# Attention and a two-layer MLP on one Trainium2 core: the first batch's second layer with three output chunks at once

## The chip, the cores and the metric

The kernel runs on one core of a Trainium2 chip. The metric is device time in microseconds (us), from start to end of the execution; lower is better. The engines concerned are TensorE (PE in the profile; its weight loads are PEld), VectorE (DVE), ScalarE (ACT), GpSimd (POOL) and SyncE (SP), which here issues DMAs. Each works through its own instructions in the order in which the program was written; they meet through semaphores.

## The reference, cut to what matters

```python
# q, k, v: (8 batches, 12 heads, 448 rows, 64)
q_n, k_n = rmsnorm(q, g_q), rmsnorm(k, g_k)
attn = softmax(q_n @ k_n.T / 8)
a = attn @ v
x = a.transpose(0, 2, 1, 3).reshape(8 * 448, 768)
h = x @ w_in                  # w_in  (768, 2048), float64
g = h - tanh(h)
return g @ w_out              # w_out (2048, 768), float64
```

The weights arrive as float64, the rest as float32. The kernel has to make float32 weights out of pairs of 32-bit words.

## The kernel before, in words

**Slots.** Attention is cut into 48 steps, one for each batch and pair of heads (six steps to a batch). A "slot" holds the work of one step s and work ahead for later ones: the softmax sums of s (`totals`), the scores of s + 1, the values of s, the transposes of q and k of s + 2 (`turn`), the norms of s + 3. The MLP is a Python generator that yields once per matmul; a slot calls `run` between its parts, and `run` draws as many MLP matmuls as the slot's share of time allows. What is drawn between two parts of a slot stands there in every engine's queue. Batch 0's first layer is drawn in slots 6 to 8, its second layer in slots 9 to 11, and batch 1's first layer begins in slot 12. In slots 6 to 11 (`early_slot`) the order is: `totals(s)`, the scores of s + 1 for key chunks 0 and 1, a quarter of the slot's matmuls, `turn(s + 2)`, a quarter, the last key chunk, `values(s)` and `divide(s)`, then four eighths of the matmuls with the softmax additions `add(s + 1)`, `add_last(s + 1)`, then `norm(s + 3)` and `norm_q(s + 3)` after them.

**The chain around `turn`.** The scores, sums, values and turns share five PSUM banks in rotation. In these slots the first bank that `turn` takes is the one that `totals` filled; it is free when DVE has taken the reciprocal of the sums (L701). The second bank that `turn` takes held the first scores; it is free when ACT has taken their exponential (L575). That exponential stands in ACT's queue behind `norm_q` (L454), which needs a power computed by POOL (L144) from what DVE reduced in `norm` (L142, L143).

**Weights.** There are 32 pieces: 0 to 15 of w_in, 16 to 31 of w_out (16 to 23 for output columns 384 to 767, two matrix rows of 128 each, in order; 24 to 31 for columns 0 to 383). A piece is loaded (L289 for w_in, L293 for w_out) into one of three raw buffers and rounded in three steps: two ACT instructions (L71, L72), three DVE instructions (L78, L79, L82), two POOL instructions (L92). `weight(to)` starts pieces up to the number `to`: it issues the ACT step of piece n and, with it, the DVE and POOL steps of piece n - 1, and then the load of a later piece. So DVE rounds a piece when the next one is started, and the list that gives `to` for each matmul of the MLP sets where in DVE's queue that work stands. In the first layer each product also catches up on the piece before, if it starts none.

**The first layer of batch 0** is 28 products (four sets of seven, Strassen's scheme), each of six matmuls of 128x128 by 128x224. Before product i, `weight(due[i])` is called: `due` rises from 8 pieces to 16 over products 0 to 13, and to 24 over products 14 to 27. When the four pieces of a set are rounded, four DVE sums (L356) are queued, one before each product.

**The second layer of batch 0** (`project_first`) is 96 matmuls of 128x128 by 128x448: six output chunks of 128 columns, each a sum over 16 rows of w_out. They are done chunk by chunk (chunks 3, 4, 5, 0, 1, 2), with f, the matrix row, innermost. Number them m = 0 to 95. Each slot draws 32 of them, 8 + 8 + 4 + 4 + 4 + 4. Three PSUM banks named `mm` are used in turn. At the end of a chunk ACT copies the bank (L1335), DVE turns it (L960), and half a chunk later four DMAs store it (L965). Pieces 24 to 31 start at m = 5, 11, 17, 23, 29, 35, 41, 47. At m = 52, 56, ... 80 DVE forms the Strassen sums of w_out (`combine_w_out`, L380 to L383, in two of six ring slots), which SP copies to DRAM four matmuls later (L387). At m = 84 and 86 `ring_load` fetches the first four weight tiles of batch 1 (L426) into the ring.

**What SP's queue holds.** All loads, stores and copies to DRAM, in program order. An entry that waits holds back the ones after it.

Of the kernel before, what the change touches and what calls it, by code (L numbers as in the profile page):

```python
# [67 lines left out]
def round_weight_a(nc, raw, dst):  # L68

    lo, hi = raw[:, :, 0], raw[:, :, 1]  # L70
    nc.scalar.activation(dst, hi.bitcast(F32), AF.Abs, scale=2.0**-16)  # L71
    nc.scalar.mul(lo, lo.bitcast(U32), 2.0**-29)  # L72
# [74 lines left out]
def bounded_path(tc, ctx, q, k, v, moe_w_in, moe_w_out, out, g_col, ident, ones, half_ones, neg_half, early):  # L147
# [17 lines left out]
    nc = tc.nc  # L165
    B, H, S, D = q.shape
    DFF, DM = moe_w_out.shape
    P = 128
    CP = S // NCH
    NP = H // 2  # L170
    CD, CF = DM // P, DFF // P
# [5 lines left out]
    EARLY, PIECES = 8, 2 * CF  # L177
    HS = S // 2
    HC, HF = CD // 2, CF // 2
    SETS = CF // 4  # L180
# [8 lines left out]
    def pool(name, **kw):  # L189
        return ctx.enter_context(tc.tile_pool(name=name, **kw))  # L190
# [18 lines left out]
    def bank_of(name):  # L209

        turns[name] += 1
        return banks[name][turns[name] % len(banks[name])]

    def mm_bank():
        return bank_of("mm")
# [48 lines left out]
    def w_out_row(f, i):  # L264
        return w_half[i][f // 2][:, f % 2]
# [35 lines left out]
    def weight_dst(n):  # L301
        return weight_piece(n)[2].rearrange("p f n -> p (f n)")
# [11 lines left out]
    def load_weights(to):  # L314

        while done[0] < min(to, PIECES) and place_free(done[0]):
            weight_load(done[0])
            done[0] += 1

    def weight(to):  # L320

        while done[1] < min(to, PIECES):
            n = done[1]
            keep_step(0, {CF - 4: 0, CF: 1, CF + HF: SETS - 1}.get(n, -1))
            round_weight_a(nc, raws[n], weight_dst(n))
            settle(n)
            done[1] = n + 1
            load_weights(n + (3 if n < EARLY - 3 else 4))
            if kept[1] < kept[0] and n >= 4 * kept[0] + 2:
                keep_weights()  # L330
            keep_step(2)
        if done[1] == PIECES:
            settle(PIECES)

    def settle(to):
        for n in range(done[2], to):
            round_weight_b(nc, raws[n], weight_dst(n))
            finish_weights(n + 1)
# [22 lines left out]
    def keep_weights():  # L361
        j = kept[1]
        to_keep.extend((j, p) for p in ORDER)
        kept[1] = j + 1
# [3 lines left out]
    def keep_step(count, all_of=-1):  # L368
        while to_keep and (count > 0 or to_keep[0][0] <= all_of):
            j, p = to_keep.pop(0)  # L370
            nc.sync.dma_start(out=w_in_dram[j, p].rearrange("p (f n) -> p f n", f=2), in_=built(j, p))
            count -= 1

    def combine_w_out(f):

        a11, a21 = (w_out_row(f, i) for i in range(2))
        a12, a22 = (w_out_row(f + HF, i) for i in range(2))
        t = [ring_slot() for _ in range(2)]
        s3, s1, s2, s4 = (t[i // 2][:, i % 2 * HALF : (i % 2 + 1) * HALF] for i in range(4))
        nc.vector.tensor_tensor(out=s1, in0=a21, in1=a22, op=ALU.add)  # L380
        nc.vector.tensor_tensor(out=s3, in0=a11, in1=a21, op=ALU.subtract)
        nc.vector.tensor_tensor(out=s2, in0=s1, in1=a11, op=ALU.subtract)
        nc.vector.tensor_tensor(out=s4, in0=a12, in1=s2, op=ALU.subtract)  # L383
        late["keep"].append(lambda: [keep_factors(3 + 2 * i, 2, f, t[i]) for i in range(2)])

    def keep_factors(n, count, f, src):
        nc.sync.dma_start(  # L387
            out=w_out_dram[:, n : n + count, :, f, :].rearrange("p k c d -> p (k c) d"),
            in_=src[:, : count * HALF].rearrange("p (k d) -> p k d", d=P),
        )  # L390

    def keep_w_out(n):

        if not CF <= n < PIECES:
            return
        f, i, src = weight_piece(n)
        if f >= HF or i == 0:
            blk = i + 1 if f >= HF else 0
            for r in range(2):
                keep_factors(blk, 1, f % HF + r, src[:, r])  # L400
# [3 lines left out]
    def ring_slot():  # L404
        n = slots[0] % SLOTS
        slots[0] += 1
        return ring[:, n * SLOT : (n + 1) * SLOT]
# [11 lines left out]
    def ring_load(to):  # L419

        for n in range(len(ring_tiles), min(to, len(ring_steps))):
            b, layer, j, p = ring_steps[n]
            t = ring_tiles[ring_steps[n]] = ring_slot()
            if layer == 0:
                assert kept[1] > j
                nc.sync.dma_start(out=t[:, : 2 * HALF], in_=w_in_dram[j, p])  # L426
            elif layer == 2 and p == 0:
                nc.sync.dma_start(out=t, in_=w_out_dram[:, BLOCKS[j], HC - 1].rearrange("p f d -> p (f d)"))
            elif layer == 2:
                n = min(2 * HB, 7 * HB - 2 * (p - 1) * HB)  # L430
                at = 2 * (p - 1) * HB
                nc.sync.dma_start(out=t[:, :n], in_=inner_dram[j][:, at : at + n])
            else:
                nc.sync.dma_start(out=t, in_=w_out_dram[:, BLOCKS[p], j].rearrange("p f d -> p (f d)"))
# [371 lines left out]
    late = {}  # L806


    due = [EARLY + (CF - EARLY) * (m + 1) // (7 * SETS // 2) for m in range(7 * SETS // 2)]
    due += [CF + HF * (m + 1) // (7 * SETS // 2) for m in range(7 * SETS // 2)]  # L810
    assert len(due) == 7 * SETS and due[-1] == CF + HF

    def part(name):
        if name == "th" and "blocks" in late:
            late["turn"] = (late.get("turn", 0) + 1) % 3
            if late["turn"] == 0:
                return late["blocks"].tile([P, 2, HS], F32, name="th_more")
        return tp.tile([P, 2, HS], F32, name=name)
# [134 lines left out]
    def store(b, n, y, o=None):  # L953

        if o is None:
            o = part("th").rearrange("p f s -> p (f s)")
        nc.vector.transpose(out=o, in_=y if b >= FIRST else y.rearrange("r (c p) -> r p c", c=NCH))  # L960

        def issue():
            for i in range(P // BL):
                d = n * P + i * BL
                nc.sync.dma_start(  # L965
                    out=out[b * S : (b + 1) * S, d : d + BL].rearrange("(j t) d -> t j d", t=BL),
                    in_=o[i * BL : (i + 1) * BL].rearrange("t (j d) -> t j d", d=BL),
                )

        late["out"].append([1 if b >= PAIRED else 2, issue])  # L970
# [33 lines left out]
    def step_out(by=1):  # L1004
        for entry in late["out"]:
            entry[0] -= by
        while late["out"] and late["out"][0][0] <= 0:
            late["out"].pop(0)[1]()
# [290 lines left out]
    def project_first(b):  # L1299

        g = late["g"]
        for fn in late["todo"]:
            fn()
        late["todo"] = []
        keep_step(0, SETS - 1)
        took = 4 * S / ENGINE_NS
        for m in range(CD * CF):
            k, f = m // CF, m % CF
            n = (k + HC) % CD
            if f == 0:  # L1310
                bank = mm_bank()
            if f == CF // 2:
                step_out(2)
            if k < HC:
                weight(CF + HF + HF * (m + 1) // (HC * CF))
            elif m < HC * CF + 2:
                keep_w_out(PIECES - 2 + m - HC * CF)
            elif (m - HC * CF) % 4 == 0 and m - HC * CF <= 4 * HF:
                for fn in late["keep"]:
                    fn()  # L1320
                late["keep"] = []
                combine_w_out((m - HC * CF) // 4 - 1)
            elif m == CD * CF - 12:
                ring_load(2)
                for fn in late["keep"]:
                    fn()
            elif m == CD * CF - 10:
                ring_load(4)
            nc.tensor.matmul(  # L1329
                bank[:, :S], lhsT=w_out_row(f, n // HC)[:, n % HC * P : (n % HC + 1) * P], rhs=g[:, f, :],  # L1330
                start=(f == 0), stop=(f == CF - 1),
            )
            if f == CF - 1:
                y = part("s2").rearrange("p f s -> p (f s)")
                nc.scalar.copy(out=y, in_=bank[:, :S])  # L1335
                store(b, n, y)
            yield took
        wp_stack.close()
        late["blocks"] = pool("blocks", bufs=1)
        late["second"] = pool("second", bufs=1)  # L1340
        late["tg"] = single_stack.enter_context(tc.tile_pool(name="tg", bufs=1))
        late["inner"] = inner_steps()
# [534 lines left out]
```

## Time and profile before

| | us |
|---|---|
| median of 3 runs | 1346.47 (1345.29 to 1346.51) |
| the profiled execution | 1346.23 |
| its span, first to last instruction | 1344.4 |
| PE busy | 1315.8 |
| DVE busy | 967.6 |
| POOL busy | 789.3 |
| ACT busy | 570.0 |
| batch 0's first layer (L851 with w_out, w_f), from | 78.2 |
| batch 0's second layer (L1329), from and to | 177.3 to 270.3 |
| batch 1's first layer, from | 278.5 |

Times are counted from the first instruction of the span. The rest of the execution's own time, 1.8 us, lies around the span. A row of a timeline gives start, duration, engine, line and operands, and in brackets how long the engine had stood idle before and for whom it waited. A float32 matmul stands in the profile as two records, so "x16" is eight matmuls.

### The profile page before, as it was taken

To read this page: it belongs to the slowest core of one execution; us is meant where nothing else is said; L and a number is where in the kernel's file an instruction comes from. 1 tells how busy PE (TensorE), PEld (TensorE's weight loads), DVE (VectorE), ACT (ScalarE), POOL (GpSimd) and SP (SyncE) were. 2 spreads that over 40 slices of the span, in tenths; PEclk is the share of its full clock that TensorE was granted. 3 is DMA by queue.
4 is the path that set the end of the run, shared out by engine and by line. 5 is a ranking of instruction groups with operands and counts; after the bars stand their busy time and mean duration, and the time that the engine had idled before them with its cause. 6 is when DMAs were issued, how large, how long until landed. Compare 5 with 4: busy or idle time off the path is not lost.

```text
span 1344.4 us, 29274 instructions
## 1 busy us (share of the span) xinstructions
PE 1315.8 (98%) x11352; PEld 1035.4 (77%) x11352; DVE 967.6 (72%) x1401; ACT 570.0 (42%) x1342; POOL 789.3 (59%) x591
## 2 busy tenths in 40 slices
PE   6999999999999999999999999999999999999997
PEld 3467854478999888688877788778887788799986
DVE  4999978756766676778887667778888577634455
ACT  7856654245333454446322345354612255311102
POOL 4766766248846256835698254934599344812661
PEclk9989999999999999999999999999999999999999
DMA  7879889979999766476655867466745775465544
GB/s 168 187 209 263 264 259 232 260 243 291 317 300 285 175 171 171 119 184 161 176 143 134 198 156 186 127 166 163 180 132 147 149 203 155 123 155 174 170 143 102
DMA packets 364743, 253.53 MB, mean 189 GB/s; under 512 B 273012, under 2 KB 303284, under 8 KB 364596
## 3 DMA queue, kind: packets, MB, share of 16 engines
q1 hardware_dynamic: 364592, 251.57, 69.0%
q8 instruction: 92, 1.51, 0.5%
q14 instruction: 55, 0.45, 0.1%
q10 hardware_dynamic: 4, 0.00, 0.0%
HBM read 205.23 MB, written 46.27 MB: 187 GB/s over the span
## 4 chain that ended last, share of the span: by engine, by line
PE 82%; DVE 5%; POOL 4%; SPq 3%; DMA 3%; issue 2%; ACT 1%; ACTq 0%; DVEq 0%; POOLq 0%
PE mm L851 38%; PE mm L1136 20%; PE sc L569 8%; PE mm L1329 5%; PE sc L635 5%; POOL u L1093 2%; PE sc L673 1%; PE sc L623 1%; POOL rr_mine L523 1%; SPq L965 1%; PE mm L673 1%; SPq L127 1%; DMA w_f<-w_inner 1%; SPq L497 1%; DMA qk_nat<-in_k_dram 1%
## 5 line engine op out<-in xcount | busy, mean ns | idle before, releaser
L851 PE MATMUL mm<-xT,w_f 128*128 128x224 f32 x1296 | 263.4, 353 | 0.0
L851 PEld LDWEIGHTS mm<-xT,w_f 128*128 128x128 f32 x1296 | 244.9, 190 | 4.8 <-issue 4.1
L569 PE MATMUL sc<-qT,kT 64*32 64x448 f32 (+1 forms) x3072 | 212.8, 499 | 2.6 <-ACT p_last L575 1.6
L851 PE MATMUL mm<-tt,w_f 128*128 128x224 f32 x1044 | 212.7, 355 | 0.8 <-DMA w_f<-w_in 0.6
L851 PEld LDWEIGHTS mm<-tt,w_f 128*128 128x128 f32 x1044 | 195.7, 190 | 16.8 <-issue 15.4
L523 POOL TENSOR_TENSOR rr_mine<-rr_mine,neg_half 128x28 f32<-128x28 f32 x33 | 161.4, 4890 | 2.8
L758 DVE TENSOR_TENSOR xT<-xT,sc 128x448 f32<-128x448 f32 x32 | 19.9, 621 | 165.1 <-PE sc L569 115.8
L899 POOL TENSOR_TENSOR gT<-s,th 128x448 f32<-128x448 f32 x44 | 57.5, 1308 | 138.0 <-ACT th L898 138.0
L1136 PE MATMUL mm<-u,w_f 128*128 128x224 f32 x672 | 137.2, 354 | 1.0 <-POOL u L1093 0.5
L1136 PE MATMUL mm<-gT,w_f 128*128 128x224 f32 (+1 forms) x496 | 132.0, 419 | 1.3 <-DVE acc L1143 0.9
L1136 PEld LDWEIGHTS mm<-u,w_f 128*128 128x128 f32 x672 | 126.1, 190 | 8.0 <-POOL u L1093 3.6
L569 PEld LDWEIGHTS sc<-qT,kT 64*32 64x32 f32 x3072 | 70.6, 106 | 69.9 <-issue 51.7
L1136 PEld LDWEIGHTS mm<-gT,w_f 128*128 128x128 f32 x496 | 93.5, 190 | 34.6 <-issue 32.0
L635 PE MATMUL sc<-p,v_nat 64*32 64x448 f32 x1120 | 110.5, 536 | 0.0
L1136 PE MATMUL mm<-g,w_f 128*128 128x224 f32 (+1 forms) x360 | 99.0, 428 | 0.0
L575 ACT ACTIVATE p<-sc 128x448 f32<-128x448 f32 x132 | 71.7, 543 | 50.4 <-PE sc L569 36.0
L899 POOL TENSOR_TENSOR g<-s,th 128x448 f32<-128x448 f32 x24 | 30.3, 1263 | 104.1 <-ACT th L898 104.1
L1136 PEld LDWEIGHTS mm<-g,w_f 128*128 128x128 f32 x360 | 67.9, 190 | 26.5 <-issue 26.0
L725 ACT COPY sum_g<-sum 32x14 f32<-32x14 f32 x280 | 56.3, 201 | 70.9 <-DVE sum L717 65.1
L1329 PE MATMUL mm<-gT,w_out 128*128 128x448 f32 x192 | 74.3, 542 | 0.0
L1093 POOL TENSOR_TENSOR u<-gT 128x448 f32<-128x448 f32 x48 | 63.5, 1344 | 11.1 <-PE mm L1136 11.1
L144 POOL TENSOR_TENSOR rr<-rr,neg_half 112x8 f32<-112x8 f32 (+1 forms) x30 | 49.1, 1664 | 26.7 <-DVE rr L143 26.1
(203 smaller groups left out, 2470.1 us busy)
## 6 DMA issues: line engine op xcount, KB each, us to landing
w_f<-w_in SPq DMA_DIRECT2D x196, 384.0 KB, 3.5
w_f<-w_inner SPq DMA_DIRECT2D x63, 512.0 KB, 3.6
w_f<-w_out SPq DMA_DIRECT2D x42, 512.0 KB, 3.8
w_raw<-in_moe_w_out_dram SPq DMA_DIRECT2D x16, 768.0 KB, 5.5
w_in<-w_out SPq DMA_DIRECT2D x21, 384.0 KB, 5.4
qk_nat<-in_q_dram SPq DMA_DIRECT2D x132, 56.0 KB, 2.7
qk_nat<-in_k_dram SPq DMA_DIRECT2D x132, 56.0 KB, 2.4
g<-w_out SPq DMA_DIRECT2D x14, 512.0 KB, 5.5
```

The costliest lines, as they stand in the source:

```text
L144: nc.gpsimd.tensor_tensor(out=r, in0=r, in1=neg_half[:rows], op=ALU.pow)
L523: nc.gpsimd.tensor_tensor(out=mine, in0=mine, in1=neg_half[:, :1].to_broadcast([P, 2 * NJ]), op=ALU.pow)
L569: nc.tensor.matmul(tiles[h][i * BL : (i + 1) * BL, :n], lhsT=kT[r, c * P + at : c * P + at + BL], rhs=qT[r, first : first + n], start=True ...
L575: nc.scalar.activation(p[:, h, c if c < 2 else 0, :], tiles[h][:, :n], AF.Exp, scale=1.0 if rr is None else rr[:, 0, 2 * c + h : 2 * c + h ...
L635: nc.tensor.matmul(av[g][i * BL : (i + 1) * BL, :S], lhsT=v_nat[keys, h, c, m * BL : (m + 1) * BL], rhs=p[keys, h], start=first, stop=True ...
L673: nc.tensor.matmul(av[n][r : r + BL, :HS], lhsT=v_nat[:, h, c, m * BL : (m + 1) * BL], rhs=p[c][:, h, n * HS : (n + 1) * HS], start=False, ...
L725: nc.scalar.copy(out=acc[h * BL : (h + 1) * BL, g], in_=part[g * BL : (g + 1) * BL, h * NJ : (h + 1) * NJ])
L851: nc.tensor.matmul(bank[:, f * HS : (f + 1) * HS], lhsT=w[:, c * width + f, :], rhs=moving[p](c), start=(first and f == 0 and c == 0), sto ...
L899: eng.tensor_tensor(out=g[:, rows, cols], in0=h, in1=th, op=ALU.subtract)
L1093: nc.gpsimd.tensor_tensor(out=u[:, half], in0=a[:, half], in1=z[:, half], op=ALU.subtract)
L1136: nc.tensor.matmul(bank[:, :n], lhsT=w(i), rhs=mv, start=(first and i == 0), stop=(i == len(moving) - 1), skip_group_check=not first,)
L1329: nc.tensor.matmul(bank[:, :S], lhsT=w_out_row(f, n // HC)[:, n % HC * P : (n % HC + 1) * P], rhs=g[:, f, :], start=(f == 0), stop=(f == C ...
```

## The change

`due` now rises evenly from 8 to 22 pieces over the 28 products. A second list, `behind`, goes on from 22 to 32 over the first 58 matmuls of the second layer. The second layer runs in two halves of 48 matmuls: three output chunks at once, each in its own bank, with the matrix row outside and the chunk inside (m = 48k + 3f + i). The three chunks of a half end at m = 45, 46, 47 and 93, 94, 95; each is copied to its own tile (`s2`, `s5`, `s1`), and the third is turned into another `s2`. `step_out()` is called every fourth matmul, and a store is issued at the second call after its chunk. The sums of w_out come at m = 58, 62, ... 86, the first ring tiles at m = 92 and 94.

```diff
-    due = [EARLY + (CF - EARLY) * (m + 1) // (7 * SETS // 2) for m in range(7 * SETS // 2)]
-    due += [CF + HF * (m + 1) // (7 * SETS // 2) for m in range(7 * SETS // 2)]
+    SOON_OUT, LAST_OUT = HF - 2, 58
+    due = [EARLY + (CF - EARLY + SOON_OUT) * (m + 1) // (7 * SETS) for m in range(7 * SETS)]
+    behind = [min(PIECES, CF + SOON_OUT + (PIECES - CF - SOON_OUT) * (m + 1) // LAST_OUT) for m in range(CD * CF)]
...
+        combined = [0]
+
+        def keep_combined(to):
+            for f in range(combined[0], min(to, HF)):
                 for fn in late["keep"]:
                     fn()
                 late["keep"] = []
+                combine_w_out(f)
+                combined[0] = f + 1
+
         for m in range(CD * CF):
-            k, f = m // CF, m % CF
-            n = (k + HC) % CD
-            if f == 0:
-                bank = mm_bank()
-            if f == CF // 2:
-                step_out(2)
-            if k < HC:
-                weight(CF + HF + HF * (m + 1) // (HC * CF))
-            elif m < HC * CF + 2:
-                keep_w_out(PIECES - 2 + m - HC * CF)
-            elif (m - HC * CF) % 4 == 0 and m - HC * CF <= 4 * HF:
-                ...
-                combine_w_out((m - HC * CF) // 4 - 1)
-            elif m == CD * CF - 12:
-                ring_load(2)
-                ...
-            elif m == CD * CF - 10:
+            k, f, i = m // (HC * CF), m % (HC * CF) // HC, m % HC
+            n = (1 - k) * HC + i
+            if m % 4 == 3:
+                step_out()
+            weight(behind[m])
+            if f == 0:
+                bank = [] if i == 0 else bank
+                bank.append(mm_bank())
+            if LAST_OUT <= m < LAST_OUT + 2:
+                keep_w_out(PIECES - 2 + m - LAST_OUT)
+            if m >= LAST_OUT - 4:
+                keep_combined((m - LAST_OUT + 4) // 4)
+            if m == CD * CF - 6:
+                ...
+            if m == CD * CF - 4:
+                ring_load(2)
+            elif m == CD * CF - 2:
                 ring_load(4)
             nc.tensor.matmul(
-                bank[:, :S], lhsT=w_out_row(f, n // HC)[:, n % HC * P : (n % HC + 1) * P], rhs=g[:, f, :],
+                bank[i][:, :S], lhsT=w_out_row(f, n // HC)[:, n % HC * P : (n % HC + 1) * P], rhs=g[:, f, :],
...
             if f == CF - 1:
-                y = part("s2").rearrange("p f s -> p (f s)")
-                nc.scalar.copy(out=y, in_=bank[:, :S])
-                store(b, n, y)
+                y = part(("s2", "s5", "s1")[i]).rearrange("p f s -> p (f s)")
+                nc.scalar.copy(out=y, in_=bank[i][:, :S])
+                store(b, n, y, part("s2").rearrange("p f s -> p (f s)") if i == 2 else None)
```

More of the change, by code (lines that the diff above doesn't have):

```diff
@@ L806, in bounded_path @@
     late = {}
-    due = [EARLY + (CF - EARLY) * (m + 1) // (7 * SETS // 2) for m in range(7 * SETS // 2)]
-    due += [CF + HF * (m + 1) // (7 * SETS // 2) for m in range(7 * SETS // 2)]
-    assert len(due) == 7 * SETS and due[-1] == CF + HF
+    SOON_OUT, LAST_OUT = HF - 2, 58
+    due = [EARLY + (CF - EARLY + SOON_OUT) * (m + 1) // (7 * SETS) for m in range(7 * SETS)]
+    behind = [min(PIECES, CF + SOON_OUT + (PIECES - CF - SOON_OUT) * (m + 1) // LAST_OUT) for m in range(CD * CF)]
+    assert due[-1] == CF + SOON_OUT and due[7 * (SETS - 1) - 1] > CF
     def part(name):
@@ L1306, in project_first @@
         took = 4 * S / ENGINE_NS
-        for m in range(CD * CF):
-            k, f = m // CF, m % CF
-            n = (k + HC) % CD
-            if f == 0:
-                bank = mm_bank()
-            if f == CF // 2:
-                step_out(2)
-            if k < HC:
-                weight(CF + HF + HF * (m + 1) // (HC * CF))
-            elif m < HC * CF + 2:
-                keep_w_out(PIECES - 2 + m - HC * CF)
-            elif (m - HC * CF) % 4 == 0 and m - HC * CF <= 4 * HF:
+        combined = [0]
+        def keep_combined(to):
+            for f in range(combined[0], min(to, HF)):
                 for fn in late["keep"]:
@@ L1321, in project_first @@
                 late["keep"] = []
-                combine_w_out((m - HC * CF) // 4 - 1)
-            elif m == CD * CF - 12:
-                ring_load(2)
+                combine_w_out(f)
+                combined[0] = f + 1
+        for m in range(CD * CF):
+            k, f, i = m // (HC * CF), m % (HC * CF) // HC, m % HC
[11 more added lines that the diff above has]
+            if m == CD * CF - 6:
                 for fn in late["keep"]:
                     fn()
-            elif m == CD * CF - 10:
+                late["keep"] = []
+            if m == CD * CF - 4:
+                ring_load(2)
+            elif m == CD * CF - 2:
                 ring_load(4)
             nc.tensor.matmul(
-                bank[:, :S], lhsT=w_out_row(f, n // HC)[:, n % HC * P : (n % HC + 1) * P], rhs=g[:, f, :],
+                bank[i][:, :S], lhsT=w_out_row(f, n // HC)[:, n % HC * P : (n % HC + 1) * P], rhs=g[:, f, :],
                 start=(f == 0), stop=(f == CF - 1),
```

## The prediction

> **What bounds the kernel now.** First the page's busy times and groups, then the windows.
>
> ```profile
> PE 1315.8 (98%) x11352; PEld 1035.4 (77%) x11352; DVE 967.6 (72%) x1401; ACT 570.0 (42%) x1342; POOL 789.3 (59%) x591
> ...
> L1329 PE MATMUL mm<-gT,w_out 128*128 128x448 f32 x192 | 74.3, 542 | 0.0
> ```
>
> PE sets the end, and the loop that is rewritten has no idle before it (last column). So the edit cannot shorten its own 96 matmuls; it can remove PE idle elsewhere, or make some. Where is there any? In the windows (length, then PE, PEld, DVE, ACT, POOL busy with counts, PE clock, DMA share, GB/s):
>
> ```profile
> 67.00:101.00 34.00, 30.70 (x362) 21.40 (x363) 33.23 (x45) 17.79 (x30) 21.69 (x17) 0.90 0.78 208
> 101.00:134.00 33.00, 30.66 (x276) 25.45 (x275) 30.73 (x44) 20.47 (x39) 22.06 (x19) 0.95 0.95 262
> 134.00:168.00 34.00, 34.00 (x303) 29.39 (x302) 31.50 (x41) 22.35 (x42) 26.72 (x19) 1.00 0.86 266
> 168.00:202.00 34.00, 34.00 (x253) 19.94 (x252) 27.20 (x33) 19.93 (x36) 22.77 (x19) 1.00 0.85 257
> 202.00:235.00 33.00, 33.00 (x213) 16.21 (x212) 29.08 (x39) 15.62 (x30) 21.07 (x19) 1.00 0.94 235
> ```
>
> Only the first layer up to 134 us has idle, with DVE nearly full and a clock below 1. The waits of PE between 55 and 140 us name the places:
>
> ```profile
> PE mm L851 <- DVE s L920: 2.6, 1, 2.6
> PE sc L467 <- DVE rs L701: 2.3, 1, 2.3
> ```
>
> The first ends at 91.53, in product 4. `due` is 8, 9, 9, 10, 10, 11 for products 0 to 5 in both versions, so this wait stays. The second is the `turn` of slot 7. PE's timeline there, then DVE's:
>
> ```profile
> 121.06 0.66 PE L467 MATMUL sc<-ident,qk_nat 128*128 128x128 f32 x4 [2.34 <-DVE rs L701]
> 121.55 0.55 PE L471 MATMUL sc<-ident,n 112*128 112x112 f32 x4
> 121.94 4.89 PE L851 MATMUL mm<-xT,w_out 128*128 128x224 f32 x16
> ```
>
> ```profile
> 116.54 0.54 DVE L78 TENSOR_SCALAR w_out<-w_out 128x768 f32<-128x768 f32 x1
> 117.11 0.56 DVE L79 TENSOR_SCALAR w_out<-w_out 128x768 int32<-128x768 int32 x1
> 117.71 0.96 DVE L82 SCALAR_TENSOR_TENSOR w_out<-w_raw,w_out 128x768 int32<-128x768 int32 x1
> 118.59 0.95 DVE L356 TENSOR_TENSOR w_f<-w_f 128x768 f32<-128x768 f32 x1
> 119.45 1.55 DVE L701 RECIPROCAL rs<-sc 128x224 f32<-128x224 f32 x1
> ```
>
> PE wanted the bank at 118.72; the reciprocal, ready since the sums ended at 111.5, stood behind a rounding and a weight sum until 121.00. The 16 records after it take 4.89 us; at the 189 ns of undisturbed ones (20.45 us for 108 in the chain) they take 3.03. The clock reads 0.57 there: 1.86 us more.
>
> [...] The trace has half-rate spells of 3.41 us, but after idles of 2.3 and 2.6 us[...]; 0.42 us at 83.7 brought none. [...] here L79 takes 0.56 us beside an idle POOL and 1.25 to 1.40 beside a busy one.
>
> **Part 1: fewer pieces ahead in the first layer.** `due` after product 8 was 13 and becomes 12. So before slot 7's reciprocal the rounding of piece 12 is gone (116.54 to 118.59: 2.05), and one L356 of three, since set 2 is complete a product later (0.87). The reciprocal ends at 118.1, before 118.72. The second bank: L143 ends some 1.3 us earlier but POOL's L92 of piece 11 moves behind a shrink, so L144 starts about 115.0 instead of 116.02 and L454 and the first exponential follow (119.68 + 0.55 becomes about 119.2); `turn` wants that bank at 119.1. Idle falls from 2.34 to 0.2, and with it the half clock: **-2.1 - 1.9 = -4.0**. Later in the layer DVE is always at least one piece lighter before a reciprocal, so the turns of slots 8 and 9 (no idle now) stay covered. If POOL's or ACT's order eats the gain, it is 0; more than -4.2 is not to be had, as the rest of the idle lies before product 6.
>
> **Part 2: the two pieces come back later.** Up to m = 47 the pace is as before (starts at m = 5, 11, 17, 23, 28, 34, 40, 46 against 5 to 47). But pieces 30 and 31 start at m = 52 and 57, so DVE rounds 29 at m = 52 and 30 and 31 at m = 57. All lies before the `turn` of slot 11, at 246.87. DVE has no gap from 228.40 (the first addition after slot 10's `divide`, which waits on PE) to 243.59, the end of slot 11's reciprocal:
>
> ```profile
> 231.04 1.01 DVE L380 TENSOR_TENSOR w_f<-w_out,w_out 128x384 f32<-128x384 f32 x1
> ...
> 241.06 0.94 DVE L960 STREAM_TRANSPOSE th<-s 128x448 f32<-128x448 f32 x1
> 242.03 1.56 DVE L701 RECIPROCAL rs<-sc 128x224 f32<-128x224 f32 x1
> ```
>
> Of this 15.2 us the change takes out one of three `combine_w_out` (2.07) and the transpose (0.97), and adds three roundings. The ten roundings from 174.6 to 226 took 2.05 to 3.8, mean 2.8. End: 243.59 - 3.04 + 3 x 2.8 = 248.95, 2.1 past what `turn` wants. At the cheapest rate it is 246.7 (no idle), at the dearest 251.9 (5.0). I take 2.1, since POOL rounds each piece just as DVE does the next. The slack now is 3.3 us, the cover that goes. The other bank is late by as much: `norm` ends near 245.3, + 1.65 (first L144) + 2.02 (L454) + 0.55 gives 248.8. Half clock after it: [...] 0.9. **+3.0**. Behind the waiting L467 stand m = 72 to 95 and the attention of slot 11; nothing else waits for them sooner, and DVE uses the pause to catch up, so the stall stays once. After it the sums of w_out (2.1 each, every 3.1 us of matmuls) run free up to slot 12: `norm` of slot 11 would end near 269, its first L144 near 270.1, before ACT's last copy (270.4 to 270.9) that stands ahead of `norm_q` in any case. So slot 12's scores, which wait for that, are not late.
>
> **Part 3: three chunks at once.** 96 matmuls, six copies, six transposes as before. Bank turnover: m = 48 and batch 1's first product reuse banks just stopped, but 4.2 us (222.1 to 226.4) and 8.2 us (270.3 to 278.5) of attention lie between on PE; the ACT steps of piece 29 (1.8), which stand between the first copy and the two others (0.53 each), fit. Without that cover m = 49 would wait about 0.8 each time. Alternating banks: no row shows 448-column matmuls doing it; products of L851, which change banks, have 0.0 idle. Bounds -1 to +1; 0.
>
> **Part 4: SP.** The first stores (12 DMAs, 2.2 to 2.8 us per four) go together at m = 55, ahead of v's loads and the copies to DRAM; all raw loads are already issued. The copies of pieces 30 and 31 to DRAM (m = 58, 59) hold SP until POOL has finished them, near 243; behind them stand slot 11's v loads, used only in slot 13, and the copies of the sums, whose ring slots are written again three sums (9 us) later. At the end the two tile loads move 8 matmuls later, behind the copies of the last sums: DVE ends these near 266 to 268, tiles are issued by 270 and take 3.5, for use at 278.5. Cover: eight microseconds of attention. Then stores of three chunks (7.5) instead of one precede the tiles of products 5 and 6: tile 6 lands near 291.5, PE wants it at 293. Taken as 0; up to +2 with that cover gone.
>
> **Sum.** -4.0 + 3.0 = -1.0 on the profiled execution of 1346.23 (span 1344.4, 1.8 around it), which lies 0.2 below the median: **1345.5**.
>
> **Rivals.**
> *Faster* (0.36): DVE's contention in part 2 is small, or its order leaves the `turn` on time. For it: the page's DVE has gaps of 2 us near 222. Against: those lie before the additions that hold the queue. Idle below 1 us, no half clock: -4.0 + 0.5 = 1342.7.
> *Slower* (0.18): the turn of slot 11 becomes a worse copy of the stall removed. Place: L467, waiting on L701. From 3.6 us per rounding: 243.59 - 3.04 + 10.8 = 251.35, idle 4.5, plus 1.9, minus 4.0 = +2.4, and 0.3 more anywhere passes the bound: 1349. Against: only one of the ten took that long.
> *Little moves* (0.46): the two stalls cancel, as summed; with the half clock +0.0, without it -1.9.
>
> **How the numbers follow.** Fast or slow counts from 0.2% (2.7 us), about what this kernel's measurement can tell from none. Cancelling reaches 1344 to 1347; range 1341.5 to 1349.7 takes in the whole gain (1342.2) and the slow case with part 4's wait in part.
>
> **What would show it.** L467 in slot 7 without its wait on L701 and no half-rate spell near 120; L467 of slot 11, some 4 us earlier than 246.87, with a new wait on L701 or L575; L1329 still 0.0 idle; `mm<-xT,w_f` of batch 1 not waiting for a ring tile. Wrong if slot 7 keeps its wait, if PE idles inside L1329, or if slot 11's turn runs on time.

## The result, and the profile after

The changed kernel takes 1348.74 us against 1345.99 for the one before (medians of 22 runs each); the ratio is 1.0022, with a 95% interval from 1.0016 to 1.0028. It is slower, by about 2.7 us. The ratio lies just past the 0.2% that the prediction set as its bound, and the interval reaches to both sides of it. The profiled execution took 1349.06 us, its span 1347.3 (before: 1346.23 and 1344.4).

The page of the kernel after, busy times and the group of the rewritten loop (its line is now L1339):

```profile
PE 1316.4 (98%) x11352; PEld 1034.4 (77%) x11352; DVE 967.0 (72%) x1401; ACT 570.6 (42%) x1342; POOL 790.9 (59%) x591
...
L1339 PE MATMUL mm<-gT,w_out 128*128 128x448 f32 x192 | 76.5, 555 | 0.0
```

PE has the same work and, inside the loop, still no idle (last column). But the loop is busy for 2.2 us longer with the same 192 records, which already points to a slower clock. The windows of the kernel after (length, then PE, PEld, DVE, ACT and POOL busy, PE clock, DMA share, GB/s) show where:

```profile
101.00:134.00 33.00, 32.70 (x295) 27.87 (x294) 29.98 (x42) 21.37 (x40) 23.00 (x19) 1.00 0.96 266
...
235.00:269.00 34.00, 30.27 (x190) 15.11 (x175) 27.79 (x46) 8.14 (x20) 11.13 (x10) 0.90 0.71 208
```

From 101 to 134 us PE's idle fell from 2.3 us to 0.3 and the clock is full. From 235 to 269, where PE was busy for all 34.00 us before at a clock of 1.00, 3.7 us are lost and the clock drops to 0.90. PE's timeline of the kernel after at both places, slot 7's `turn` and slot 11's:

```profile
117.92 0.60 PE L467 MATMUL sc<-ident,qk_nat 128*128 128x128 f32 x4
118.82 0.60 PE L471 MATMUL sc<-ident,n 112*128 112x112 f32 x4 [0.30 <-ACT p L575]
119.26 3.21 PE L852 MATMUL mm<-xT,w_out 128*128 128x224 f32 x16
...
246.41 1.12 PE L467 MATMUL sc<-ident,qk_nat 128*128 128x128 f32 x4 [3.73 <-DVE rs L701]
247.32 0.95 PE L471 MATMUL sc<-ident,n 112*128 112x112 f32 x4
248.06 8.44 PE L1339 MATMUL mm<-gT,w_out 128*128 128x448 f32 x16
```

The same eight matmuls in the kernel before, from its timeline:

```profile
247.70 6.19 PE L1329 MATMUL mm<-gT,w_out 128*128 128x448 f32 x16
```

So the wait of slot 7 is gone, with its half clock (16 records in 3.21 us instead of 4.89). The same wait has come up in slot 11, longer, and followed by 6.8 us of half clock instead of 3.4 (the clock reads 0.97 from 242 to 246 us, 0.50 to 250 and 0.57 to 253, which makes 6.8 us at half). L471, which needs the other bank, waits for nothing, so the chain through `norm` does not hold the turn. It ends only just before: the exponential that frees that bank (the first of L575) starts at 245.58, and the reciprocal ends at 246.35.

Comparing the start of the same PE record in both traces gives the account. Before product 6 the new kernel is 0.6 us ahead by the accidents of one execution (the trace of before has a spell of half clock at 67.5 us, 16 records of L696 in 1.57 us, that the kernel after does not have: 0.96). After slot 7 it is 4.3 ahead (3.7 of them from the turn and the clock), and stays there up to 242 us. Slot 11's turn costs 3.9 and the half clock after it 3.1: 2.6 behind. Batch 1 adds 0.6, and the span ends 2.9 longer.

DVE's timeline of the kernel after, from the first addition after slot 10's `divide` to slot 11's reciprocal, shortened to what grew:

```profile
223.76 1.09 DVE L600 TENSOR_TENSOR rows<-p 128x896 f32<-128x896 f32 x1
...
229.11 1.96 DVE L613 TENSOR_TENSOR rows<-rows,p_last 64x448 f32<-64x448 f32 x2
...
233.87 0.55 DVE L78 TENSOR_SCALAR w_out<-w_out 128x768 f32<-128x768 f32 x1
234.46 1.26 DVE L79 TENSOR_SCALAR w_out<-w_out 128x768 int32<-128x768 int32 x1
235.75 1.66 DVE L82 SCALAR_TENSOR_TENSOR w_out<-w_raw,w_out 128x768 int32<-128x768 int32 x1
237.33 0.55 DVE L380 TENSOR_TENSOR w_f<-w_out,w_out 128x384 f32<-128x384 f32 x1
237.80 1.36 DVE L381 TENSOR_TENSOR w_f<-w_out,w_out 128x384 f32<-128x384 f32 x1
239.08 1.36 DVE L382 TENSOR_TENSOR w_f<-w_f,w_out 128x384 f32<-128x384 f32 x1
...
244.79 1.56 DVE L701 RECIPROCAL rs<-sc 128x224 f32<-128x224 f32 x1
```

In the kernel before, L613 took:

```profile
234.03 1.26 DVE L613 TENSOR_TENSOR rows<-rows,p_last 64x448 f32<-64x448 f32 x2
```

The stretch takes 22.6 us where it took 15.2. Counted from start to start, the three roundings take 2.9, 2.8 and 3.5, L613 0.7 more than before, the first sum 3.7 instead of 3.0.

### The profile page after: what moved, and what is told of

Its sections match the earlier page's. It is cut to its first block, busy times and chain, and to the rows that moved or that the text cites. A ratio compares the mean times of both kernels' runs of the same rounds, so it can differ in the third digit from the quotient of the medians.

```text
span 1347.3 us, 29273 instructions
## 1 busy us (share of the span) xinstructions
PE 1316.4 (98%) x11352; PEld 1034.4 (77%) x11352; DVE 967.0 (72%) x1401; ACT 570.6 (42%) x1342; POOL 790.9 (59%) x591
## 4 chain that ended last, share of the span: by engine, by line
PE 80%; DVE 8%; POOL 4%; DMA 2%; SPq 2%; issue 2%; ACT 1%; DVEq 0%; POOLq 0%; ACTq 0%
PE mm L852 39%; PE mm L1137 20%; PE sc L569 8%; PE sc L635 6%; POOL u L1094 2%; PE mm L1339 2%; PE sc L623 1%; PE sc L673 1%; POOL rr_mine L523 1%; DVE rows L613 1%; SPq L127 1%; DVE w_out L82 1%; PE mm L673 1%; DMA w_f<-w_in 1%; DVE rows L606 1%
## 5 line engine op out<-in xcount | busy, mean ns | idle before, releaser
L900 POOL TENSOR_TENSOR gT<-s,th 128x448 f32<-128x448 f32 x44 | 57.3, 1306 | 129.3 <-ACT th L899 129.3
L575 ACT ACTIVATE p<-sc 128x448 f32<-128x448 f32 x132 | 71.9, 545 | 50.3 <-PE sc L569 35.9
L900 POOL TENSOR_TENSOR g<-s,th 128x448 f32<-128x448 f32 x24 | 30.3, 1261 | 104.1 <-ACT th L899 104.1
L1339 PE MATMUL mm<-gT,w_out 128*128 128x448 f32 x192 | 76.5, 555 | 0.0
L1094 POOL TENSOR_TENSOR u<-gT 128x448 f32<-128x448 f32 x48 | 63.4, 1342 | 11.1 <-PE mm L1137 11.1
L92 POOL TENSOR_TENSOR w_out<-w_out,w_raw 128x384 int32<-128x384 int32 x40 | 48.4, 1230 | 33.0 <-issue 7.6
```

What stands on the lines that cost most here:

```text
L92: nc.gpsimd.tensor_tensor(out=bits[:, part], in0=bits[:, part], in1=raw[:, part, 0], op=ALU.add)
L575: nc.scalar.activation(p[:, h, c if c < 2 else 0, :], tiles[h][:, :n], AF.Exp, scale=1.0 if rr is None else rr[:, 0, 2 * c + h : 2 * c + h ...
L900: eng.tensor_tensor(out=g[:, rows, cols], in0=h, in1=th, op=ALU.subtract)
L1094: nc.gpsimd.tensor_tensor(out=u[:, half], in0=a[:, half], in1=z[:, half], op=ALU.subtract)
L1339: nc.tensor.matmul(bank[i][:, :S], lhsT=w_out_row(f, n // HC)[:, n % HC * P : (n % HC + 1) * P], rhs=g[:, f, :], start=(f == 0), stop=(f = ...
```

## The experiments

Each kernel was timed beside the kernel before on the same chip; ratios are to that. "PE's lead" is how much earlier a PE record starts than the same one in the trace of before. Waits and leads are of one profiled execution of each kernel, times are medians.

**Theory:** the loss is slot 11's turn, since DVE has too much in its queue before L701. **Rivals:** the new loop itself costs time (banks, bundled copies and stores); ACT's and POOL's chain through `norm` holds the turn; the late ring tiles cost time.

### The loop alone

The new loop, with the old list (16 pieces ahead, the rest over 48 matmuls) and sums from m = 52:

```diff
-    SOON_OUT, LAST_OUT = HF - 2, 58
-    due = [EARLY + (CF - EARLY + SOON_OUT) * (m + 1) // (7 * SETS) for m in range(7 * SETS)]
+    SOON_OUT, LAST_OUT = HF, 48
+    due = [EARLY + (CF - EARLY) * (m + 1) // (7 * SETS // 2) for m in range(7 * SETS // 2)]
+    due += [CF + HF * (m + 1) // (7 * SETS // 2) for m in range(7 * SETS // 2)]
...
-            if m >= LAST_OUT - 4:
-                keep_combined((m - LAST_OUT + 4) // 4)
+            if m >= LAST_OUT:
+                keep_combined((m - LAST_OUT) // 4)
```

> The new loop (three chunks at once, bundled stores, later sums' tail unchanged from the changed kernel's form) with the old pacing: 16 pieces ahead, pieces 24 to 31 over 48 matmuls, sums of w_out from m = 52. Theory (only the place of the roundings in DVE's queue matters): slot 7's wait of L467 on L701 is back at 2 to 3 us with its half clock, slot 11's turn has none, time within 0.1% of the kernel before. Rival (the loop itself, its alternating banks, bundled copies and stores cost time): slower than before by 1 us or more, with L1339 or batch 1's first products waiting.

Measured: ratio 0.9996 (0.9988 to 1.0004), 1346.09 us. Slot 7's wait on L701 is back with half clock (four records in 1.11 us that take 0.60 in the kernel after), in PE's timeline of this kernel:

```profile
120.81 1.11 PE L467 MATMUL sc<-ident,qk_nat 128*128 128x128 f32 x4 [2.61 <-DVE rs L701]
```

Slot 11's turn has none, and nothing waits in the loop. The order of the matmuls, the alternating banks and the bundled copies cost nothing that these runs show. What the change does to the time comes from the lists: when pieces are rounded and, with them, when w_out is summed.

### The POOL step left out for three pieces

```diff
-            round_weight_c(nc, raws.pop(done[2]), weight_dst(done[2]))
+            raw = raws.pop(done[2])
+            if done[2] < 29:
+                round_weight_c(nc, raw, weight_dst(done[2]))
```

> The changed kernel without the POOL step of pieces 29, 30 and 31 (their low words are left out, so these weights are not rounded fully). Theory (the term was mis-sized because POOL's step lengthens the DVE rounding beside it): the three roundings take 2.1 us each instead of 2.8 to 3.5, the first sum 2.2 instead of 3.6 and L613 1.3 instead of 2.0; L701 of slot 11 ends 4 us sooner and the turn waits less than 0.5 us; 1342 to 1343. Rival (DVE's amount of work alone is too much): the wait stays above 2 us and the time near the changed kernel's.

Two of the roundings and the first sum in DVE's timeline of this kernel:

```profile
231.06 0.56 DVE L78 TENSOR_SCALAR w_out<-w_out 128x768 f32<-128x768 f32 x1
231.65 0.56 DVE L79 TENSOR_SCALAR w_out<-w_out 128x768 int32<-128x768 int32 x1
232.25 0.96 DVE L82 SCALAR_TENSOR_TENSOR w_out<-w_raw,w_out 128x768 int32<-128x768 int32 x1
...
235.65 0.55 DVE L383 TENSOR_TENSOR w_f<-w_out,w_out 128x384 f32<-128x384 f32 x1
```

The second and third rounding take 2.1 us, the sum 2.1, L613 1.3, the stretch 18.2 instead of 22.6, and slot 11's turn does not wait. (The first rounding still takes 2.9, as in the kernel after, where POOL's L803, to 227.77, stands beside its first two instructions, 1.01 and 0.90 us.) That is the theory's part, and it shows the size of POOL's share: 4.4 us with the same DVE instructions. But the time is 0.9992 (0.9984 to 1.0000), not the 1342 to 1343 expected. PE enters batch 1's first layer at 274.82, 3.7 us ahead of before, and enters batch 2's at 435.42, 0.7 behind; between them PE waits 3.7 us for ring tiles. So there is a second effect, which the theory did not have: in batch 1 a lead is taken back.

### The sums later

```diff
-            if m >= LAST_OUT - 4:
-                keep_combined((m - LAST_OUT + 4) // 4)
+            if m >= 66:
+                keep_combined((m - 63) // 3)
```

> The changed kernel with the eight sums of w_out at m = 66, 69, ... 87 instead of 58, 62, ... 86: two of them (2.1 and 3.6 us of DVE) leave the stretch before slot 11's turn. Theory (DVE's queue before slot 11's reciprocal is 3.7 us too long): the reciprocal ends 5.7 us sooner, L467 of slot 11 does not wait, no half clock after it, and the whole gain of slot 7 stays: about 1342, 0.3% below before. Rival (ACT's and POOL's chain through norm is what holds the turn, or the sums only move the wait to slot 12): 1345 or more, with PE waiting at L471 on L575 or in slot 12.

Measured: 1.0009 (1.0002 to 1.0015), 1348.54 us. The turn of slot 11 waits no longer (0.3 us at L471), and PE enters batch 1 at 275.69, 2.8 us ahead. But the time is far from the theory's 1342. The rival named slot 12, and PE does wait 0.9 us more for ACT there. The larger loss neither had: PE stands in batch 1's first layer for a tile, as its timeline shows:

```profile
291.98 2.51 PE L852 MATMUL mm<-tt,w_f 128*128 128x224 f32 x12 [1.57 <-DMA w_f<-w_in]
```

In batch 1 such waits add up to 5.1 us, and it enters batch 2 at 438.17, 3.4 us behind. In SP's queue the first four tiles stand behind the copies of the later sums and are issued from 265.08 (before: two at 253.36, two at 262.37); that this is the reason was not tested apart.

### The pieces sooner

```diff
-    SOON_OUT, LAST_OUT = HF - 2, 58
+    SOON_OUT, LAST_OUT = HF - 2, 48
...
-            if m >= LAST_OUT - 4:
-                keep_combined((m - LAST_OUT + 4) // 4)
+            if m >= 54:
+                keep_combined((m - 54) // 4)
```

> The changed kernel with the ten last pieces paced over 48 matmuls instead of 58 (sums as there): pieces 30 and 31 start at m = 43 and 47, so all roundings lie before slot 10's divide. Theory (the three late roundings are the excess): slot 11's turn does not wait; about 1342. Rival (raw loads cannot keep this pace, ACT stands waiting for piece 31 ahead of the third copy): PE waits inside L1339 at m = 50, or the roundings slip past divide all the same; 1345 or more.

Measured: 1.0020 (1.0011 to 1.0030), 1350.11 us, not 1342. The turn of slot 11 does not wait, but the rival is right on the cause of the new loss: ACT waits for raw pieces, and the exponentials behind them come late. ACT's timeline, then PE's:

```profile
221.64 0.91 ACT L71 ACTIVATE w_out<-w_raw 128x768 f32<-128x768 f32 x1 [0.75 <-DMA w_raw<-in_moe_w_out_dram]
...
223.66 0.78 ACT L575 ACTIVATE p_last<-sc,rr 128x224 f32<-128x224 f32 x2
```

```profile
224.16 1.37 PE L569 MATMUL sc<-qT,kT 64*32 64x448 f32 x14 [1.90 <-ACT p_last L575]
```

The place differs from the one expected: the scores of slot 10, 1.9 us of wait and slower matmuls behind it (32 records of L1339 in 13.55 us, against 12.29 in the kernel with the sums later), not m = 50. That takes the whole lead (PE enters batch 1 0.4 us behind). Another 2.0 us go in batch 1, where PE waits 1.5 us for DVE (L900); why is open.

### Fifteen pieces ahead, and three variants of what follows

One piece fewer in the late stretch, with slot 7's queue unchanged (`due` is still 12 after product 8):

```diff
-    SOON_OUT, LAST_OUT = HF - 2, 58
+    SOON_OUT, LAST_OUT = HF - 1, 52
...
-            if m >= LAST_OUT - 4:
-                keep_combined((m - LAST_OUT + 4) // 4)
+            if m >= 54:
+                keep_combined((m - 54) // 4)
```

> The changed kernel with 15 pieces ahead and the other nine over 52 matmuls, sums as there (from m = 58): one rounding fewer before slot 11's turn, and slot 7's reciprocal has the same work before it as in the changed kernel. Theory of slot 11: the turn of slot 11 waits less than 0.5 us, PE reaches batch 1's first layer 3.5 to 4.5 us before the kernel before. Theory of batch 1 (transfers of batch 1's layers cannot start or run earlier, so PE then waits for ring tiles): the lead is gone by batch 2, time within 0.15% of before. Rival (the lead holds to the end): 1342.5.

The same, with the inner factors spread (and this edit alone on the kernel before as a control):

```diff
-            if b and b <= PAIRED:
+            late["inner_turn"] = not late.get("inner_turn", False)
+            if b == PAIRED or b and b < PAIRED and late["inner_turn"]:
                 inner_step()
```

> As g1_fifteen_ahead, and the preparation of the inner w_out factors (fetches, GpSimd sums, copies to DRAM) takes a step only after every second product of batch 1 and the rest in batch 2's first layer, so about half of its transfers leave batch 1's layers. Theory (batch 1's layers are bound by the bytes moved there): no PE wait for ring tiles in batch 1, the 4 us of lead stay, 1342 to 1343. Rival (it is the late start of SP's queue, not the bytes): lead lost as in g1_fifteen_ahead.

> The kernel before with the same spreading of the inner factors. There PE has no wait for a tile in batch 1, so all theories expect the time of before within 0.1%; if it is faster by more than 1 us, batch 1 had hidden losses, and g2_fifteen_spread must be read against this one.

Fifteen ahead, with the sums closer together and the tiles eight matmuls earlier ("early tiles"):

```diff
+            if m >= 58:
+                keep_combined(sum(at <= m for at in (58, 62, 64, 67, 70, 73, 76, 79)))
-            if m == CD * CF - 6:
+            if m == CD * CF - 14:
...
-            if m == CD * CF - 4:
+            if m == CD * CF - 12:
                 ring_load(2)
-            elif m == CD * CF - 2:
+            elif m == CD * CF - 10:
```

> As g1_fifteen_ahead, with the sums of w_out at m = 58, 62, 64, 67, 70, 73, 76, 79 and the first ring tiles issued at m = 84 and 86, where the kernel before has them. Theory of the late start (SP's queue enters batch 1 late because tiles stand behind the last sums): most of the lead stays, 1343. Rival (bytes, or the bundled stores): as g1_fifteen_ahead.

| | enters batch 1 | enters batch 2 | time | ratio (95%) |
|---|---|---|---|---|
| before | 278.50 | 434.74 | 1346.73 | 1 |
| changed | 281.12 | 437.92 | 1348.74 | 1.0022 (1.0016 to 1.0028) |
| 15 ahead | 275.67 | 434.46 | 1345.37 | 0.9991 (0.9983 to 0.9999) |
| 15 ahead, spread | 277.35 | 433.58 | 1345.19 | 0.9985 (0.9979 to 0.9992) |
| before, spread | 278.32 | 434.56 | 1347.23 | 1.0000 (0.9991 to 1.0009) |
| 15 ahead, early tiles | 275.06 | 431.29 | 1343.60 | 0.9977 (0.9969 to 0.9986) |

(The changed kernel's row is from its own comparison, where before had 1345.99; the others share one. The two entries are of one execution each; the one of the last row was the fastest of its twelve, 1341.70.) With 15 ahead the turn of slot 11 waits for nothing. PE loses 1.2 us just before it, at the sums' matmuls (L696), which wait for the additions (L613), since two roundings now stand in front of these:

```profile
235.20 1.13 PE L696 MATMUL sc<-rows,ones 128*32 128x224 f32 x8 [0.53 <-DVE rows L613]
...
244.04 0.60 PE L467 MATMUL sc<-ident,qk_nat 128*128 128x128 f32 x4
```

So PE arrives 2.8 us early, less than the 3.5 to 4.5 expected. It loses 2.5 of them in batch 1, the last at its end, in PE's timeline of that kernel:

```profile
434.46 2.51 PE L852 MATMUL mm<-xT,w_f 128*128 128x224 f32 x12 [0.81 <-DMA w_f<-w_in]
```

With early tiles PE has no wait for a tile in batch 1 and brings its whole lead of 3.4 us to batch 2; the median is 1.8 us below that of 15 ahead. With the inner factors spread PE has no such wait either, but in its one profile it had only 1.2 us of lead to lose, and no gain over 15 ahead shows (the intervals overlap; 1342 to 1343 was expected). The control shows that spreading alone is worth nothing when PE is not early. The bytes alone do not decide: from 302 to 437 us the DMA share in four windows is 0.90 to 0.93 in the kernel without three POOL steps, where PE waits 3.7 us for tiles in batch 1, and 0.92 to 0.96 in the kernel before, where it waits for none. SP's timeline shows what the late tail moves: the first fetch for the inner factors, which stands behind the tiles and the bundled stores, in before and with 15 ahead:

```profile
270.42 0.83 SPq L1022 DMA_DIRECT2D g<-w_out  x2
```

```profile
275.59 0.90 SPq L1023 DMA_DIRECT2D g<-w_out  x2
```

With early tiles it starts at 272.41. Sums and tiles were moved together, so which of them holds the queue is not separated; and the loop alone, with the changed kernel's late tiles and this fetch at 275.55, gives back 1.0 us in batch 1 although it enters it only 0.5 ahead. The version with early tiles beats both kernels.

### The tail alone, and one sum fewer

The changed kernel (14 ahead, 58) with the tail of the early-tiles version:

> The changed kernel (14 ahead, the rest over 58) with only the tail of g4_fifteen_tiles: sums at m = 58, 62, 64, 67, 70, 73, 76, 79, tiles at m = 84 and 86. Two sums and three roundings still stand before slot 11's turn. Theory (slot 11's stall sets the loss, the late tiles cost only a PE that is early): L467 waits 3 to 4 us there, half clock after it, time within 0.1% of the changed kernel, 1348 to 1349. Rival (the late tiles cost the changed kernel too): 1346 or less.

Measured: 1.0017 (1.0010 to 1.0023), 1348.84 us, with 3.7 us of wait at slot 11's L467, as expected. In the changed kernel the late tail costs nothing that shows: PE arrives late anyway.

The changed kernel with one of two sums taken out of the stretch:

```diff
-                keep_combined((m - LAST_OUT + 4) // 4)
+                keep_combined(sum(at <= m for at in (62, 66, 69, 72, 75, 78, 82, 86)))
```

> The changed kernel with the sums at m = 62, 66, 69, 72, 75, 78, 82, 86: one of two (some 2 to 3.6 us of DVE) leaves the stretch before slot 11's turn, tiles late as in the changed kernel. Theory: the wait there falls from 3.7 to between 0 and 1.7 us, without half clock, PE reaches batch 1 2.5 to 4 us before the kernel before, and gives 2 us or more of it back waiting for tiles: 1345 to 1346.5. Rival (half clock even after so short a wait): 1347 or more.

Measured: 0.9991 (0.9983 to 0.9999), 1345.46 us. In PE's timeline the wait is 0.6 us, and the four records after it take 0.66 (1.12 in the changed kernel); the mean granted clock of its profiled run is 0.998, against 0.995 there:

```profile
244.35 0.66 PE L467 MATMUL sc<-ident,qk_nat 128*128 128x128 f32 x4 [0.56 <-DVE rs L701]
```

PE arrives at 276.46 (2.0 ahead) and enters batch 2 at 434.07 (0.7 ahead) after 1.1 us of waiting for a tile. With one DVE sum fewer in the stretch the whole loss is gone.

Fifteen ahead with early tiles and one sum fewer before the turn (62, 64, 66, 68, 71, 74, 77, 80):

> g4_fifteen_tiles with the sums at m = 62, 64, 66, 68, 71, 74, 77, 80: only one before slot 11's turn, where g4 still waited 1.2 us. Theory: that wait goes, 1 us faster than g4: 1342.5. Rival (the denser sums delay slot 11's divide or the tiles): as g4 or slower.

Measured: 0.9986 (0.9978 to 0.9994), 1344.91 us. No gain over the version with 58 shows; the intervals overlap. The expectation rests on a misreading: the 1.2 us of waits in the version with 58 (L467 at 117.60, L471 at 118.87) belong to slot 7's turn, and slot 11's had none to lose.

## Why the prediction was wrong

It forecast 1345.5, a change too small to tell with a lean to faster; the kernel is 2.7 us slower. The time lies in the range given, near the case called *slower*, which had 0.18. That case named the place, the instruction and the reciprocal it waits on. That its total fits is in part luck: its idle was too long (4.5 us, measured 3.7) and its half clock too cheap (1.9, measured 3.1).

*Part 1, fewer pieces ahead* (-4.0): right. L467 of slot 7 waits for nothing, L471 0.3 us, the half clock is gone; 3.7 us in the trace. The loop alone, with the old lists, brings the wait back.

*Part 2, the two pieces come back later* (+3.0): the step that failed. Mechanism, place and sign were right; two terms of the sum were mis-sized. The stall was put at 2.1 and is 3.7. The stretch was to grow by 5.4 us and grew by 7.4. A third of the difference is the roundings themselves (9.1 instead of 8.4). The rest was left out: the POOL steps slow the DVE work around the roundings too, L613 by 0.7 and the first sum by 0.7 more than in before. (Of the 2.0 us, 0.4 were covered: the turn came that much later after the start of the stretch.) Without those POOL steps the stretch is 4.4 us shorter. The half clock was put at 0.9, an estimate halfway between none and the 1.9 that slot 7's 3.4 us of it cost; after an idle of 3.7 it lasted 6.8 us, and cost 3.1. Part 2 was +7.0 instead of +3.0, and the sum would have been +3.0 with it, near the 2.9 of the spans. The working for the other bank also has a slip: 245.3 + 1.65 + 2.02 + 0.55 is 249.5, not 248.8; nothing hung on it, since that bank did not hold the turn.

*Part 3, three chunks at once* (0): right; the loop alone has the time of before.

*Part 4, SP* (0, up to 2): right for the changed kernel, where PE arrives late (its own tail or the early one: 1348.74 and 1348.84), and wrong for a PE that is early. The rival *faster*, 1342.7, let a lead of 3.5 us pass through batch 1. With the late tail, leads of 2.0 to 3.7 us on entering batch 1 were 0.7 or less on entering batch 2; with early tiles, leads of 3.0 and 3.4 passed whole. With this tail even a slot 11 whose turn does not wait gives only 0.1%, as the run without three POOL steps (0.9992) and 15 ahead (0.9991) do.

On POOL the runs show this: the same three DVE instructions take 2.1 us without POOL's step (from 231.06 to 233.12 in the kernel without it) and up to 3.5 beside it (from 233.87 to 237.33 in the kernel after). But not every record of POOL lengthens the DVE work beside it: L144, 3.6 us from 241.99 in the kernel after, stood beside the second sum, which took 2.2, and L79 took 0.56 not only beside an idle POOL, as the prediction has it, but beside L144 as well (117.11 in the kernel before). By what means POOL's step lengthens the DVE work was not shown.

Open: when a wait of PE is followed by half clock. The 2.5 us wait of product 4 was followed by it in before, changed, sums later, pieces sooner and without the POOL step (its eight records took 2.18 to 3.35 us), and not in the loop alone (1.78). A wait of 1.6 us at slot 6's turn (L467) was followed by none in the five of these six that have it (the eight records after the turn took 1.69 in each).

## What to carry to other kernels

When work is moved along an engine's queue, add up that queue from the last point where it surely waits to the next instruction that PE needs, with the durations it has beside the work that moves with it (2.9, 2.8 and 3.5 us here for roundings of 2.1), and price the half clock as well as the idle (3.1 us here, after an idle of 3.7). A stall removed on the bounding engine was worth little here where the tiles of the next stage came no earlier (leads of 2.0 to 3.7 us became 0.7 or less): before counting the lead to the end, look at what stands ahead of that stage's first transfers in the queue that issues them. The DMA share did not tell here; it was no higher where a lead was lost waiting for tiles (0.90 to 0.93) than where PE waited for none (0.92 to 0.96). Pacing lists are worth a sweep in single steps: one piece or one sum turned +0.2% into -0.1%, and 15 pieces with earlier sums and tiles into -0.2%.

## What the runs showed that was not expected

In the changed kernel an idle of 3.7 us on PE was followed by 6.8 us of half clock, so the stop cost nearly twice its length (3.9 and 3.1 us). And a DVE sum of four instructions of 128x384 took 2.1 us with POOL idle (from 235.32 in the kernel before) and 3.7 with POOL's weight step beside it (from 237.33 in the kernel after; L92 from 237.54 to 240.02).
